# One spectrum tile with two channels interleaved, filled by one copy per step, in a long-convolution and mixture-of-experts kernel

## The chip, the core and the metric

The kernel runs on one core of one Trainium2 chip. The metric is the device time of one execution in microseconds, the median over runs. One execution was also recorded by the hardware profiler; the durations below are from that record. The engines are named as in the profile: PE is TensorE's matmuls and PEld its weight loads, DVE is VectorE, ACT is ScalarE, POOL is GpSimd and SP is SyncE, which issues most DMAs.

## What is computed

For each of four batches of 10048 positions with 128 channels, `u = x * v` is convolved along the positions with a filter that a small network makes, and the result is multiplied by x. Each of the 40192 rows then goes to one of 16 experts.

```python
h_filt = np.maximum(pos_emb @ w1, 0.0) @ w2 * np.exp(-0.01 * pos)[:, None]
Uf = np.fft.rfft(x * v, n=2 * S, axis=1)
Hf = np.fft.rfft(h_filt, n=2 * S, axis=0)
y = np.fft.irfft(Uf * Hf[None], n=2 * S, axis=1)[:, :S, :]
rows = (x * y).reshape(B * S, D)
...
g_idx = np.argmax(rows @ w_group, axis=1)          # a group of experts
e_idx = np.argmax(xg @ w_expert[g], axis=1)        # an expert of the group
ye = np.maximum(xg[mask_e] @ w1[g, e], 0.0) @ w2[g, e]
out[tok_idx] = combined[:, None] * ye
```

## The kernel before

The transform is done in two factors, 157 frequencies by 128 places; by symmetry 79 frequencies (NB) are kept. The work of one batch passes three stages, and each batch's last stage is merged with the next batch's first.

**Forward stage.** `dft_blocks` (L408) works on steps of three channels (GD). One step multiplies the folded input `eo` by the constants `fa` into a PSUM tile `psa`: for each channel two products, one for each half of the partitions. The result holds 158 values per channel, 79 frequencies by two parts. ScalarE copies it to SBUF in two instructions: the lower 64 frequencies (KM) to the tile `z`, 384 elements, and the upper 15 to the tile `zr`, 90 elements. In the filter's own transform and in batch 0, VectorE does some of these copies. What feeds a step is in `product` and `fold`: a DMA loads x and v of three channels (`xv`, five buffers), VectorE multiplies them (L467), ScalarE negates a half (L478), VectorE adds (L480).

**Middle stage.** `middle` and `dft_positions` take two frequencies at a time across all channels (moving operand `z[:, :, k]`, L497), multiply with the filter's spectrum, and `back` (L667) transforms back (L673) and has ScalarE copy the result into the same places of `z` or `zr` (L680).

**Inverse stage.** `turned` (L683) turns twelve channels at a time: three transposes of `zr` (L692), each with four channels' 32 upper values, and twelve of `z` (L695), one for each channel with 128 lower values. They fill four PSUM tiles `pt`, which ScalarE copies to four tiles `tt` (L697). The pool of `pt` has three buffers, so the last four transposes wait until the first `pt` has been copied. `inverse_rest` (L701) multiplies the first `tt` with the constants `fi` into two PSUM tiles `po` (L707), and `inverse_blocks` (L712) adds the products of the other three (L728) for each run of six channels. ScalarE then makes `oo` from `po` in two instructions (L737, L738), VectorE adds (`yt`, L743) and multiplies by x (`xy`, L745).

In the loop of `conv`, the inverse stage of one batch and the forward stage of the next run merged: for each twelve channels, one `turned`, one `inverse_rest`, two `inverse_blocks` and four forward steps. This document calls such a round a **turn**, from one burst of L707 on TensorE to the next. There are ten full turns and a short one in each of the three merged stages, then the last inverse stage of batch 3 without forward steps, then the experts.

Each engine works through its list in order. The lists come from a scheduler, which places an instruction by its dependences; those marked with `keep_in_program_order` (the copies to `z`, the negations L478, VectorE's L467 and L480) keep the order of the code among themselves, while the copies of `pt` and the two `oo` instructions may be placed between them as the scheduler sees fit.

## Time and profile before

| | |
|---|---|
| median of 3 runs | 1946.3 us (1944.04 to 1946.36) |
| the profiled execution | 1945.94 us, its span 1944.2 us |
| PE, PEld busy | 1852.0 us (95%), 1567.9 us (81%) |
| DVE, ACT, POOL busy | 1458.0 us (75%), 1317.4 us (68%), 1086.7 us (56%) |
| forward stage of the filter, of batch 0 | about 43 to 78 us, 118 to 178 us |
| merged stages | about 247 to 341, 440 to 535 and 643 to 742 us |
| last inverse stage | about 848 to 912 us, then the experts to the end |

A busy share is a mean over stages with different limits, and the records of neighbouring matmuls overlap, so that TensorE can show as busy while nothing new is issued. For a stage that repeats, the time from one start of the same instruction to the next says more: it contains every wait. The timeline views give those starts.

### The profile page before, as it was taken

The page shows a single profiled execution, that of the slowest core. Times are in us where ns is not written, and L with a number is a line of the kernel's source. Part 1 is how long each engine was busy: PE and PEld are TensorE (multiplying, and loading weights), DVE is VectorE, ACT ScalarE, POOL GpSimd, SP SyncE. Part 2 cuts the span into 40 slices and gives each one's busy share as a digit, 9 for nine tenths or more (in the row PEclk, how much of TensorE's full clock was granted, in tenths as well). Part 3 has the DMA queues.
Part 4 walks back from the last instruction along what each step waited for, and adds up shares of the span by engine and source line. Part 5 has one row for each costly group of instructions (what it writes and reads, how often), then busy time and mean ns, then how long its engine had stood idle before and what let it go on. Part 6 is the DMA issues. An engine that isn't in the chain of part 4 may idle for free.

```text
span 1944.2 us, 44476 instructions
## 1 busy us (share of the span) xinstructions
PE 1852.0 (95%) x14494; PEld 1567.9 (81%) x14494; DVE 1458.0 (75%) x3102; ACT 1317.4 (68%) x3017; POOL 1086.7 (56%) x1225
## 2 busy tenths in 40 slices
PE   8988999989999899978899999999999999999997
PEld 7966878778877687766788888888888888899997
DVE  6577767688768976893789777777777777778885
ACT  6653378447843685446777777777777777788886
POOL 3237710664799568967255556666664333355554
PEclk9999999999999999999899999999999999999999
DMA  4599976988998799857653344444343222234332
GB/s 145 199 283 252 306 188 191 350 267 263 282 326 289 233 265 343 302 186 241 218 194 112 118 128 127 164 133 131 121 131 98 90 94 97 79 119 128 122 121 77
DMA packets 234433, 365.19 MB, mean 188 GB/s; under 512 B 29687, under 2 KB 113634, under 8 KB 234192
## 3 DMA queue, kind: packets, MB, share of 16 engines
q1 hardware_dynamic: 198960, 286.90, 47.9%
q0 software_dynamic: 25728, 59.82, 8.9%
q10 hardware_dynamic: 9504, 15.54, 2.9%
q8 instruction: 117, 1.92, 0.4%
q14 instruction: 124, 1.02, 0.2%
HBM read 272.15 MB, written 91.03 MB: 187 GB/s over the span
## 4 chain that ended last, share of the span: by engine, by line
PE 66%; DVE 10%; DMA 4%; ACT 4%; issue 3%; POOL 2%; SPq 0%; ACTq 0%; DVEq 0%; POOLq 0%
PE ph L1334 8%; PE ph L1336 8%; PE py L1354 8%; PE ph L1335 8%; PE py L1356 8%; PE py L1355 8%; PE psb L497 4%; PE pbp L673 3%; PE ptm L1368 2%; PE px L1289 2%; PE po L728 2%; DMA xv<-xv_in 2%; PE po L707 2%; DMA bt<-c_b 1%; DVE t L660 1%
## 5 line engine op out<-in xcount | busy, mean ns | idle before, releaser
L1343 DVE SCALAR_TENSOR_TENSOR hl<-ph,hh 128x512 fp32r<-128x512 f32 x656 | 450.4, 687 | 172.1 <-ACT hh L1342 167.2
L1380 POOL DMA_INDIRECT out<-os,to x328 | 324.6, 990 | 384.1 <-ACT os L1375 309.6
L1342 ACT ACTIVATE hh<-ph 128x512 fp32r<-128x512 f32 x656 | 395.4, 603 | 157.5 <-PE ph L1336 134.8
L378 POOL DMA_INDIRECT prow<-stg,adr x316 | 326.3, 1032 | 122.6 <-issue 53.9
L1334 PE MATMUL ph<-xh,wh 128*128 128x512 f32 (+1 forms) x808 | 301.2, 373 | 2.2 <-ACT wh L1316 2.2
L1336 PE MATMUL ph<-xh,wl 128*128 128x512 f32 (+1 forms) x808 | 284.4, 352 | 0.0
L1354 PE MATMUL py<-hh,wh 128*128 128x512 f32 (+1 forms) x808 | 283.5, 351 | 0.0
L1335 PE MATMUL ph<-xl,wh 128*128 128x512 f32 (+1 forms) x808 | 283.4, 351 | 0.0
L1356 PE MATMUL py<-hh,wl 128*128 128x512 f32 (+1 forms) x808 | 283.0, 350 | 0.0
L1355 PE MATMUL py<-hl,wh 128*128 128x512 f32 (+1 forms) x808 | 282.2, 349 | 0.0
L661 POOL TENSOR_TENSOR y<-t 128x256 f32<-128x256 f32 (+1 forms) x160 | 121.1, 757 | 141.0 <-DVE t L660 136.4
L412 PE MATMUL psa<-fa,eo 96*64 96x158 f32 x2048 | 182.1, 305 | 12.6 <-POOL eo L486 5.7
L680 ACT COPY z<-pbp 128x512 f32<-128x512 f32 x128 | 74.8, 585 | 160.5 <-PE pbp L673 155.7
L673 PE MATMUL pbp<-y,bp 128*128 128x256 f32 x632 | 164.7, 384 | 12.7 <-POOL y L664 12.7
L497 PE MATMUL psb<-z,bt 128*128 128x256 f32 x640 | 161.8, 384 | 10.6 <-DMA bt<-c_b 3.9
L1336 PEld LDWEIGHTS ph<-xh,wl 128*128 128x128 f32 x808 | 153.6, 190 | 21.2 <-DVE wl L1323 0.2
L1355 PEld LDWEIGHTS py<-hl,wh 128*128 128x128 f32 x808 | 153.2, 190 | 20.9
L1356 PEld LDWEIGHTS py<-hh,wl 128*128 128x128 f32 x808 | 153.1, 189 | 20.7
L1354 PEld LDWEIGHTS py<-hh,wh 128*128 128x128 f32 x808 | 153.0, 189 | 20.3
L412 PEld LDWEIGHTS psa<-fa,eo 96*64 96x64 f32 x2048 | 143.2, 138 | 32.0 <-POOL eo L486 9.2
L1334 PEld LDWEIGHTS ph<-xh,wh 128*128 128x128 f32 x808 | 154.0, 191 | 17.3 <-ACT wh L1316 2.4
L1335 PEld LDWEIGHTS ph<-xl,wh 128*128 128x128 f32 x808 | 154.5, 191 | 14.9
(233 smaller groups left out, 3771.4 us busy)
## 6 DMA issues: line engine op xcount, KB each, us to landing
ws<-m_w SPq DMA_DIRECT2D x202, 256.0 KB
ht<-hspec SPq DMA_DIRECT2D x156, 256.0 KB
xv<-xv_in SPq DMA_DIRECT2D x131, 288.0 KB
bt<-c_b SPq DMA_DIRECT2D x95, 256.0 KB
bp<-c_bp SPq DMA_DIRECT2D x76, 256.0 KB
xyd<-xy SPq DMA_DIRECT2D x76, 256.0 KB
stg<-xyd SPq DMA_DIRECT2D x76, 256.0 KB
xg<-prow SPq DMA_DIRECT2D x63, 260.0 KB
```

The costliest lines, as they stand in the source:

```text
L378: ins = self.nc.gpsimd.indirect_dma_start(self.d["prow"], bass.IndirectOffsetOnAxis(ap=u.adr[:, t : t + 1], axis=0), u.rows[:, t - u.t0], ...
L412: ins = nc.tensor.matmul(ps[hs, i], eo[:, i, hs], self.fa[:, h], start=True, stop=True)
L497: nc.tensor.matmul(ps[:, i].rearrange("p s d -> p d s"), bt[:, i], self.frequency(k0 + i, 1)[:, :, 0], start=True, stop=True,)
L1334: k.fix(nc.tensor.matmul(ph[:, j], wh, self.xh, start=True, stop=False))
L1335: k.fix(nc.tensor.matmul(ph[:, j], wh, self.xl, start=False, stop=False))
L1336: k.fix(nc.tensor.matmul(ph[:, j], wl, self.xh, start=False, stop=True))
L1342: k.fix(nc.scalar.activation(hh, ph, AF.Relu))
L1343: k.fix(nc.vector.scalar_tensor_tensor(hl, ph, 0.0, hh.bitcast(F32), ALU.max, ALU.subtract))
L1354: k.fix(nc.tensor.matmul(self.py, wh, hh, start=(c == 0), stop=False))
L1355: k.fix(nc.tensor.matmul(self.py, wh, hl, start=False, stop=False))
L1356: k.fix(nc.tensor.matmul(self.py, wl, hh, start=False, stop=(c == NC - 1)))
L1380: ins = k.nc.gpsimd.indirect_dma_start(k.d["out"], bass.IndirectOffsetOnAxis(ap=self.to[:, h : h + 1], axis=0), o, None, bounds_check=k.nt ...
```

## The change

`z` and `zr` become one tile of 64 channel pairs by 160 values by two channels, so that a channel's neighbouring values stand 8 bytes apart. A forward step now covers one of the two places of its pairs and needs one copy of 3 x 158 elements instead of two. So that steps pair up, the last eight channels are done in four steps of two instead of two of three and one of two: 44 steps instead of 43. The upper values of a pair are interleaved now and are turned by ordinary products with the identity, two for each place of `pt`, each giving 64 partitions: six products instead of three transposes per turn. The transposes of the lower values read their weights with a step of two elements. `dft_positions` and `back` read and write runs of 4 and 8 elements instead of 2 and 4. The constants `fi` and the order of the channels on the host follow.

```diff
-        self.z = zp.tile([128, D, KM, 2], F32, name="z")
-        self.zr = zp.tile([128, D, 16, 2], F32, name="zr")
-        nc.vector.memset(self.zr[:, :, NB - KM :], 0.0)
+        self.z = zp.tile([128, D // 2, 2 * KM + 32, 2], F32, name="z")
+        nc.vector.memset(self.z[:, :, 2 * NB :], 0.0)
...
+PARTS = groups(120, GD) + [(d0, 2) for d0 in range(120, 128, 2)]
...
-        for name, to, at in (
-            ("z", main, ps[:, :n, : 2 * KM]),
-            ("zr", rest, ps[:, :n, 2 * KM :]),
-        ):
-            ins = copy(to, at)
+        pair = d0 // (2 * n) * n
+        ins = copy(self.z[:, pair : pair + n, : 2 * NB, d0 // n % 2], ps[:, :n])
...
-                ps[:, i].rearrange("p s d -> p d s"),
+                ps[:, i].rearrange("p s (a t) -> p a s t", t=2),
                 bt[:, i],
-                self.frequency(k0 + i, 1)[:, :, 0],
+                self.frequency(k0 + i, 1),
...
-        for s, m in [(None, n // 4)] + groups(n, 4):
+        m = n // 4
+        for g in range(-1, m):
             pt = self.psT.tile([128, 4, 128], F32, tag="pt", name="pt")
-            for i in range(m):
-                if s is None:
-                    src = self.zr[:, d0 + 4 * i : d0 + 4 * i + 4].rearrange("p d k s -> p (d k s)")
-                    nc.tensor.transpose(pt[:, i], src, self.ident)
+            for i in range(m if g < 0 else 4):
+                if g < 0:
+                    for run, rs in enumerate(HALVES):
+                        src = self.z[:, d0 // 2 + run * m + i, 2 * KM :].rearrange("p k t -> p (k t)")
+                        nc.tensor.matmul(pt[rs, i], src, self.ident, start=True, stop=True)
                 else:
-                    src = self.z[:, d0 + s + i].rearrange("p k s -> p (k s)")
+                    src = self.z[:, d0 // 2 + i // 2 * m + g, : 2 * KM, i % 2]
                     nc.tensor.transpose(pt[:, i], src, self.ident)
```

The code around the merged loop is the same, but the scheduler gives the lists another order. ScalarE's list in the first merged stage, between the `oo` of a turn's first run (first two rows) and the copies of the next `pt`; before, from every second turn (xv is the negation L478, z and zr the copies of a forward step):

```order
L737 ACTIVATE oo<-po 64x474
L738 COPY oo<-po 64x474
L478 ACTIVATE xv<-xv 96x3x64
L425 COPY z<-psa 128x384
L425 COPY zr<-psa 128x3x30
L737 ACTIVATE oo<-po 64x474
L738 COPY oo<-po 64x474
L478 ACTIVATE xv<-xv 96x3x64
L425 COPY z<-psa 128x384
L425 COPY zr<-psa 128x3x30
L478 ACTIVATE xv<-xv 96x3x64
```

In the turns between, the list before has the order that the changed kernel has in every turn of this stage:

```order
L737 ACTIVATE oo<-po 64x474
L738 COPY oo<-po 64x474
L478 ACTIVATE xv<-xv 96x3x64
L424 COPY z<-psa 128x3x158
L723 DMA xo<-x_out 128x474
L478 ACTIVATE xv<-xv 96x3x64
L424 COPY z<-psa 128x3x158
L737 ACTIVATE oo<-po 64x474
L738 COPY oo<-po 64x474
L478 ACTIVATE xv<-xv 96x3x64
L424 COPY z<-psa 128x3x158
L697 COPY tt<-pt 128x384
```

The second run's `oo` has moved behind the second negation of the turn. TensorE's list in the same stage, before, for two turns from the transposes on (psa are the forward products, po with 64x158 the burst L707):

```order
L692 MATMUL pt<-ident,zr 128x128 x3
L695 MATMUL pt<-ident,z 128x128 x8
L412 MATMUL psa<-fa,eo 64x158 x5
L695 MATMUL pt<-ident,z 128x128 x4
L412 MATMUL psa<-fa,eo 64x158
L707 MATMUL po<-fi,tt 64x158 x12
L728 MATMUL po<-fi,tt 64x79 x12
L412 MATMUL psa<-fa,eo 64x158 x12
L728 MATMUL po<-fi,tt 64x79 x12
L412 MATMUL psa<-fa,eo 64x158 x6
L692 MATMUL pt<-ident,zr 128x128 x3
L695 MATMUL pt<-ident,z 128x128 x8
```

And in the changed kernel, where eight turns of the first merged stage read alike:

```order
L692 MATMUL pt<-ident,z 64x128 x6
L695 MATMUL pt<-ident,z 128x128 x8
L416 MATMUL psa<-fa,eo 64x158 x5
L695 MATMUL pt<-ident,z 128x128 x4
L416 MATMUL psa<-fa,eo 64x158
L707 MATMUL po<-fi,tt 64x158 x12
L728 MATMUL po<-fi,tt 64x79 x12
L416 MATMUL psa<-fa,eo 64x158 x12
```

Before, every second turn has nine forward products ahead of the last four transposes and none behind them; now every one of these eight has five ahead and one behind. The ninth has three and three. In the second merged stage one turn has three and three, one five and one, and seven have seven ahead and none behind; in the third, four have seven ahead, one five and one, and the first half is irregular as before. At the end of each merged stage the last copy to `z`, on which the next L497 waits, now stands behind the last two `oo` instructions on ScalarE; before it stood ahead of them. 

## Rows read from the trace of the kernel before

**Rows 1.** Busy time by stretch: PE, PEld, DVE, ACT, POOL, clock, DMA share, GB/s.

```profile
250.00:330.00 80.00, 76.97 (x1227) 66.26 (x1225) 56.20 (x106) 66.23 (x181) 0.00 (x0) 1.00 0.67 182
445.00:530.00 85.00, 81.00 (x1274) 69.94 (x1270) 68.15 (x141) 68.69 (x187) 54.05 (x57) 0.98 0.97 280
645.00:735.00 90.00, 84.99 (x1309) 72.22 (x1309) 74.28 (x172) 69.38 (x187) 56.23 (x52) 0.99 0.95 261
```

**Rows 2.** Timeline of TensorE, two turns: start, length, line, operation, count, idle before.

```profile
268.82 1.04 PE L707 MATMUL po<-fi,tt 64*64 64x158 f32 x24
...
276.29 0.66 PE L695 MATMUL pt<-ident,z 128*128 128x128 f32 x4 [0.19 <-ACT tt L697]
276.87 0.48 PE L412 MATMUL psa<-fa,eo 96*64 96x158 f32 x2
277.29 1.04 PE L707 MATMUL po<-fi,tt 64*64 64x158 f32 x24
...
282.46 0.55 PE L692 MATMUL pt<-ident,zr 128*128 128x128 f32 x3
...
285.76 0.66 PE L695 MATMUL pt<-ident,z 128*128 128x128 f32 x4 [0.39 <-ACT tt L697]
286.35 0.90 PE L707 MATMUL po<-fi,tt 64*64 64x158 f32 x20
```

**Rows 3.** Timeline of ScalarE in the second of these turns.

```profile
279.40 0.56 ACT L737 ACTIVATE oo<-po 64x474 f32<-64x474 f32 x1 [0.95 <-PE po L728]
279.98 0.55 ACT L738 COPY oo<-po 64x474 f32<-64x474 f32 x1
...
282.44 0.36 ACT L478 ACTIVATE xv<-xv 96x192 f32<-96x192 f32 x1 [1.03 <-DVE xv L467]
282.71 0.46 ACT L425 COPY z<-psa 128x384 f32<-128x384 f32 x1
283.07 0.23 ACT L425 COPY zr<-psa 128x90 f32<-128x90 f32 x1
283.33 0.56 ACT L737 ACTIVATE oo<-po 64x474 f32<-64x474 f32 x1
...
285.10 0.23 ACT L425 COPY zr<-psa 128x90 f32<-128x90 f32 x1
285.23 1.94 ACT L697 COPY tt<-pt 128x384 f32<-128x384 f32 x4
```

**Rows 4.** Timeline of VectorE there, ahead of the negation at 282.44.

```profile
281.24 0.65 DVE L745 TENSOR_TENSOR xy<-yt,xo 128x474 f32<-128x474 f32 x1
```

**Rows 5.** Timeline of ScalarE in the first of the two turns.

```profile
273.09 0.56 ACT L737 ACTIVATE oo<-po 64x474 f32<-64x474 f32 x1
```

**Rows 6.** Groups by line, 0 to 1100 us: busy us, mean ns, idle before and releasers.

```profile
L497 PE MATMUL psb<-z,bt 128*128 128x256 f32 x640 | 161.8, 384 | 10.6 <-DMA bt<-c_b 3.9 <-DVE hs L635 2.4 <-DVE t L663 2.2
L425 ACT COPY z<-psa 128x384 f32<-128x384 f32 x181 | 85.3, 471 | 55.3 <-PE psa L412 55.1
L425 ACT COPY zr<-psa 128x90 f32<-128x90 f32 x181 | 43.7, 241 | 0.0
```

**Rows 7.** One line's instructions, L866: shortest/median/longest ns; it writes every second element.

```profile
L866 DVE TENSOR_SCALAR en<-idc x4: 193/458/797, 414.0 to 1008.0; 128x79 f32<-128x79 f32 x4
```

**Rows 8.** Timeline of TensorE in the last inverse stage.

```profile
879.36 1.04 PE L695 MATMUL pt<-ident,z 128*128 128x128 f32 x8
881.10 0.66 PE L695 MATMUL pt<-ident,z 128*128 128x128 f32 x4 [0.70 <-ACT tt L697]
```

**Rows 9.** Timeline of TensorE and ScalarE at the end of the first merged stage.

```profile
341.25 2.88 PE L497 MATMUL psb<-z,bt 128*128 128x256 f32 x12
...
341.34 0.43 ACT L737 ACTIVATE oo<-po 64x316 f32<-64x316 f32 x1
```

**Rows 10.** Timeline of TensorE, forward products of a step group in the same stage.

```profile
279.12 1.78 PE L412 MATMUL psa<-fa,eo 96*64 96x158 f32 x24
280.74 0.99 PE L728 MATMUL po<-fi,tt 128*64 128x79 f32 x24
```

More of the change, by code (lines that the diff above doesn't have):

```diff
@@ L98, in make_consts @@
         both[:NB, 1 - swap] = (2 * swap - 1) * w * np.sin(ang)
-        rest = np.zeros((4, 32, 2, NB))
-        for i in range(4):
-            rest[i, :, i % 2] = both[KM:].reshape(32, NB)
+        rest = np.zeros((2, 32, 2, 2, NB))
+        for i in range(2):
+            rest[:, :, i, i] = both[KM:].reshape(32, NB)
         sign = 1 - 2 * swap
@@ L138, with step_of @@
 OUTS = groups(120, GI) + [(120, 4), (124, 4)]
+PARTS = groups(120, GD) + [(d0, 2) for d0 in range(120, 128, 2)]
+def step_of(d0):
+    return d0 // GD if d0 < 120 else 40 + (d0 - 120) // 2
 def channels():
     order = []
-    for i, (d0, n) in enumerate(OUTS):
-        first = d0 - i % 2 * n
-        order += [first + 4 * (c // 2) + i % 2 * 2 + c % 2 for c in range(n)]
+    for d0, n in OUTS:
+        order += [d0 + c % 2 * (n // 2) + c // 2 for c in range(n)]
     return np.array(order)
@@ L247, in conv @@
                 xy = xyp.tile([128, NB, D], F32, tag="xy", name=f"xy{b - 1}")
-            parts = groups(D, GD) if not last else []
+            parts = PARTS if not last else []
             if b == 1:
@@ L406, in dft_blocks @@
         nc = self.nc
-        pool, tag = (self.psA, "ps") if b not in ("h", 0) or d0 // GD % 2 else (self.psT, "pt")
+        pool, tag = (self.psA, "ps") if b not in ("h", 0) or step_of(d0) % 2 else (self.psT, "pt")
         ps = pool.tile([128, GD, 2 * NB], F32, tag=tag, name="psa")
@@ L417, in dft_blocks @@
         copy = nc.vector.tensor_copy if other else nc.scalar.copy
-        main = self.z[:, d0 : d0 + n].rearrange("p d k s -> p d (k s)")
-        rest = self.zr[:, d0 : d0 + n].rearrange("p d k s -> p d (k s)")[:, :, : 2 * (NB - KM)]
-        for name, to, at in (
-            ("z", main, ps[:, :n, : 2 * KM]),
-            ("zr", rest, ps[:, :n, 2 * KM :]),
-        ):
-            ins = copy(to, at)
-            self.in_turn(b, ins)
-            self.tc.declare_no_dep(ins.ins, group=f"{name}{b}", reason="every step has channels of its own")
-            self.tc.add_to_no_dep_group(f"{name}{b}", ins.ins)
+        pair = d0 // (2 * n) * n
+        ins = copy(self.z[:, pair : pair + n, : 2 * NB, d0 // n % 2], ps[:, :n])
+        self.in_turn(b, ins)
+        self.tc.declare_no_dep(ins.ins, group=f"z{b}", reason="every step has channels of its own")
+        self.tc.add_to_no_dep_group(f"z{b}", ins.ins)
         self.pace = ins
     def run_ahead(self, b, i, made, folded):
-        parts = groups(D, GD) if b < self.nbat else []
+        parts = PARTS if b < self.nbat else []
         while len(made) < min(len(parts), i + AHEAD + 2):
@@ L488, in fold @@
         self.in_turn(b, sub.tensor_tensor(eo[:, :n, 64:128], lo, hi, ALU.subtract))
-        return b, eo, d0, n, d0 // GD % 5 == 4 or d0 // GD == 41
+        return b, eo, d0, n, step_of(d0) % 5 == 4 or d0 == 124
     def dft_positions(self, k0, n, bt, other=False):
@@ L506, in frequency @@
     def frequency(self, k, n):
-        z, k = (self.z, k) if k < KM else (self.zr, k - KM)
-        return z[:, :, k : k + n]
+        return self.z[:, :, 2 * k : 2 * (k + n)]
     def parts(self, pool, src, tag, bufs=1, lo=None):
@@ L598, in filter @@
                 break
-        for d0, n in groups(D - FH, GD):
-            self.dft_blocks("h", eo[1][:, d0 : d0 + n], FH + d0, n, d0 // GD % 2 > 0)
+        for d0, n in (p for p in PARTS if p[0] >= FH):
+            self.dft_blocks("h", eo[1][:, d0 - FH : d0 - FH + n], d0, n, step_of(d0) % 2 == 0)
         halves[1].close()
@@ L679, in back @@
             )
-        self.pace = nc.scalar.copy(self.frequency(k0, n), po[:, :, :n])
+        self.pace = nc.scalar.copy(self.frequency(k0, n), po[:, :, : 2 * n])
     def turned(self, d0, n):
```

22 lines of the change are left out of this document (11 added, 11 removed).

## The prediction

> **What bounds the kernel now.** The change touches the forward copies, the middle stage's operands and the transposes. I read the busy shares by stretch first. In the three merged stages TensorE shows 77 of 80, 81 of 85 and 85 of 90 us [rows 1], ScalarE 66 to 69 and VectorE 56 to 74. By that table TensorE is the bound, but its records overlap, so I went to the timelines and asked how long one turn takes and what it is made of.
>
> A turn from one L707 burst to the next takes 8.47 us (268.82 to 277.29) and the following one 9.06 (277.29 to 286.35) [rows 2], and the two alternate, 8.77 on the mean. The long turn can be taken apart without a remainder, along a loop through three engines. From L707 it is 2.11 us until ScalarE starts the first run's `oo` (279.40), behind L728. From there 3.04 us to the second negation at 282.44, which waited 1.03 us for VectorE [rows 3]: VectorE had to wait for `oo`, then add and multiply (L745 at 281.24, [rows 4]) before the product that the negation reads. Then 0.89 us for negation, z and zr, 1.90 us for the second run's `oo`, a negation, z and zr, and 0.53 us until the first `pt` is copied and its buffer free (285.23 to 285.76) [rows 3, 2]. The last four transposes start there, and L707 follows 0.59 us later. 2.11 + 3.04 + 0.89 + 1.90 + 0.53 + 0.59 = 9.06. TensorE itself stands idle for 0.39 us before the four transposes, more than that behind the modelled ends.
>
> In the short turn ScalarE does the second run's `oo` before that negation: it starts 4.27 us after L707 (273.09) [rows 5, 2], against 6.04 in the long one (283.33). VectorE's work then hides behind `oo`, and this pays for the 1.00 us from transposes to L707 (276.29 to 277.29), where a forward product stands between. So a turn is bound by the loop, not by any engine's sum, and the two lists of ScalarE in the section on the change are its two versions.
>
> **The change part by part.** The forward copies: z and zr take 471 and 241 ns on the mean, 181 times on ScalarE [rows 6]. The slope between 384 and 90 elements is 0.78 ns, so 474 elements take about 0.54 us; an `oo` copy of 474 takes 0.55 [rows 3], and I take that. Busy time falls by 0.16 us a step. What the loop gains is less, since a copy overlaps the one before: z and zr take 0.62 us from start to start up to `oo` (282.71 to 283.33) and 0.49 up to the `pt` copy (0.36 and 0.13) [rows 3]. One copy would take 0.58 and 0.43. The two copies that lie on the loop save 0.04 and 0.06, the other two of a turn lie in waits. A long turn becomes 8.96.
>
> The order: every turn of the changed kernel has ScalarE's long-turn order. That costs 8.96 - 8.77 = 0.19 us a turn by itself. Where one forward product stands behind the four transposes, L707 follows 1.00 instead of 0.59 us after their start, so 9.37; with three, four more records of 67 ns (24 in 1.62 us, 279.12 to 280.74, [rows 10]) make it 9.64. First merged stage: eight turns of 9.37 and one of 9.64, 8 x 0.60 + 0.87 = 5.7 us. Second: seven of 8.96 and one of 9.37, 7 x 0.19 + 0.60 = 1.9; the one with three falls in a turn that waits for VectorE anyway. Third: 4 x 0.19 + 0.60 = 1.4; for its irregular half I take nothing. Sum 9.0 us. The bounds are 4 us, if the product behind the transposes costs nothing, and 12, if the irregular turns pay too.
>
> The products with the identity: a single-pass transpose takes about 0.10 us ((1.04 - 0.55) / 5, from eight and three in a burst, [rows 8, 2]), so three take 0.3. Six float products are recorded as twelve; L412, also on half the columns each, makes 67 ns for 158 columns, so 54 for 128 and 0.65 in all: 0.35 us more per turn. This lies beside the loop. From L707 to the turn's L692 it is 5.17 us (277.29 to 282.46); with 0.65 for the products, 0.9 for eight transposes and 0.7 to 0.9 for forward products TensorE reaches the last four transposes at 7.4 to 7.7 us, while the loop lets them go at 8.37. In the last inverse stage TensorE idles 0.70 us at that point [rows 8], which covers it too. Without that cover it would cost 0.35 x 42 turns, 15 us. It has no cover at the four starts of these stages, where L692 waits for the last copy of the middle stage: 1.4 us.
>
> The Trainium skill, page "TensorE: Matmul & The Clock Gate", section "Terms", speaks against this part: it says that the transpose mode is four times as fast for FP32 as not using it. By it the six products would take up to 1.3 us per turn with two halves side by side, about 1 us more than the transposes, and the sum would be some 8 us higher.
>
> The end of a merged stage: L497 starts at 341.25, ahead of the last `oo` at 341.34 (0.43 us, two of them) [rows 9]. Now the copy that it waits for comes behind them, so it starts up to 0.9 us later, three times. What follows is partly bound by VectorE's routing work, so I take half, 1.4 us; the ends are 0 and 2.7.
>
> The rest I cost at nothing. The filter's forward stage is bound by TensorE's unchanged products, batch 0 by loads. L497 reads its moving operand in runs of two elements at present, and twelve of its records follow each other in 2.88 us [rows 9], 0.23 us for 256 columns less the last one's 0.38; that is 0.9 ns a column, near the 0.8 of the transposes with contiguous operands, so longer runs have little to gain and I take nothing. The 44th step's extra negation, copy and load lie in waits; uncovered, about 1 us a batch.
>
> Weights with a step of two elements and copies that write every second element are not in this trace in just that form. The nearest row is L866, where VectorE writes every second element: 79 elements in 193 ns at best, 458 at the median [rows 7], so a full rate is possible and a loss not excluded. L497's moving operand, in runs of two at wide steps, is read at full rate [rows 6]. I take no loss. Upper bound, double time per element: 0.4 us for each of the two copies on the loop, 0.8 x 30 = 24 us, and 0.1 us for each of the four transposes on it, 13 us there and 4 in the last stage.
>
> The Trainium skill, page "SBUF — State Buffer", section "Door 1: The DMA port swizzle", gives lines of 16 bytes and full bandwidth when two accesses fall in one line, as with a step of two fp32. By that rule this loss would have a chance of 0.03 rather than the 0.10 below; the median of L866 does not bear it out clearly.
>
> Sum against the profiled execution, 1945.94 us: 9.0 + 1.4 + 1.4 = 11.8, so 1957.7; I say 1958. That execution lies 0.4 us below the median of the runs.
>
> **Rivals.** *ScalarE's sum sets the turn (faster).* If ScalarE's list were what limits the merged stages, all 129 pairs of copies there would return their 0.16 us: -21 us, 1925, or about 1938 with the order's cost on top. It decides only if ScalarE has no waits left in a turn. For it: ScalarE works without idle time from `oo` to the copies in the short turn. Against it: 0.95 and 1.03 us of idle time in the long one [rows 3]. Chance 0.16, between 1925 and 1941.
>
> *The order hardly matters (no change).* If TensorE started L707 beside the forward product, all turns would take 8.96, 22 x 0.19 = 4 us more; with the ends of the stages absorbed and a little gained elsewhere, 1943 to 1950. The short turn's 1.00 us speaks against it. Chance 0.13.
>
> *Every second element is dear.* 1974 (weights alone) to 1999. Chance 0.10.
>
> *The products outgrow their cover.* If they took twice as long, 1.3 us, TensorE would reach the last transposes at 8.1 to 8.4 us with the same forward products and later where these wait: up to 0.3 us in 30 turns, 9 us, and 0.3 in ten of the last stage, 1960 to 1970. The page's factor for the transpose mode would be that case. Twelve records of L412's kind [rows 10] speak against it. Chance 0.05.
>
> **How the numbers follow.** The forecast, 1951 to 1965, has 0.56. Slower by over 0.2% (3.9 us, about what a measurement here can tell from no change) are the forecast, the dear elements and the products: 0.71. Within: 0.13. Faster: 0.16. The range 1940 to 1974 holds the forecast, no change, the products' case, the upper edge of the faster case and the lower edge of the dear elements, some 0.8.
>
> **What would show it.** The turns of the first merged stage at 9.37 us each without alternation, those of the second at 8.96; the second negation waiting over 1 us for L467 in each; the forward copy at 0.55 us; transposes still at 0.10 to 0.11 us apart, L692's twelve in 0.65; the last inverse stage's turns unchanged. Turns below 8.77 would overthrow the loop; turns of 9.06 behind a forward product would overthrow the 0.41; a copy of 0.9 us or transposes 0.2 apart would show the dear elements.

## The result, and the profile after

The changed kernel takes 1966.86 us (median of 4 runs, 1961.41 to 1971.23), the kernel before 1945.17 us beside it (4 runs, 1942.9 to 1946.36): a ratio of 1.0106, with a 95% interval of 1.0077 to 1.0135. It is slower, as forecast, and by more than the 11.8 us of the sum: 2 us above the 1951 to 1965 of the forecast and inside the 1940 to 1974 of the range. The profiled execution is the slowest of the four, 1971.23 us with a span of 1969.4.

To see where the time went I cut both spans at the first and the last record of L707 in each merged stage. The column "again" is a second trace of the same changed kernel (first experiment below).

| stretch | before | after | difference | difference, again | predicted |
|---|---|---|---|---|---|
| start to first L707 | 250.80 | 252.07 | +1.27 | +3.12 | +0.35 |
| first merged stage | 87.52 | 94.21 | +6.69 | +6.69 | +5.7 |
| middle | 104.45 | 104.04 | -0.41 | -0.53 | +0.8 |
| second merged stage | 90.34 | 95.25 | +4.91 | +6.84 | +1.9 |
| middle | 113.25 | 113.28 | +0.03 | +2.01 | +0.8 |
| third merged stage | 93.31 | 104.54 | +11.23 | +0.98 | +1.4 |
| middle | 108.24 | 108.77 | +0.53 | +0.48 | +0.8 |
| last inverse stage | 63.72 | 64.87 | +1.15 | +0.37 | 0 |
| rest | 1032.56 | 1032.37 | -0.19 | -0.16 | 0 |
| span | 1944.2 | 1969.4 | +25.2 | +19.8 | +11.8 |

Busy shares tell little of this. The row of busy times on the page, after (us, share of the span, instructions):

```profile
PE 1878.1 (95%) x14878; PEld 1601.0 (81%) x14878; DVE 1459.9 (74%) x3080; ACT 1314.5 (67%) x2840; POOL 1086.8 (55%) x1226
```

TensorE's share is what it was, and ScalarE has 177 instructions less but only 2.9 us less of busy time. The turns do tell it. TensorE's timeline of one turn of the first merged stage, after (start, length, engine, line, operation, count, idle time before it and what ended that):

```profile
289.98 1.04 PE L707 MATMUL po<-fi,tt 64*64 64x158 f32 x24
...
295.05 0.83 PE L692 MATMUL pt<-ident,z 128*64 128x128 f32 x12
295.81 1.23 PE L695 MATMUL pt<-ident,z 128*128 128x128 f32 x8
296.97 1.02 PE L416 MATMUL psa<-fa,eo 96*64 96x158 f32 x10
298.38 0.74 PE L695 MATMUL pt<-ident,z 128*128 128x128 f32 x4 [0.40 <-ACT tt L697]
299.06 0.48 PE L416 MATMUL psa<-fa,eo 96*64 96x158 f32 x2
```

And ScalarE's in the same turn:

```profile
292.09 0.56 ACT L737 ACTIVATE oo<-po 64x474 f32<-64x474 f32 x1 [1.03 <-PE po L728]
...
295.13 0.36 ACT L478 ACTIVATE xv<-xv 96x192 f32<-96x192 f32 x1 [1.04 <-DVE xv L467]
295.39 0.58 ACT L424 COPY z<-psa 128x474 f32<-128x474 f32 x1
295.99 0.57 ACT L737 ACTIVATE oo<-po 64x474 f32<-64x474 f32 x1
...
297.87 1.94 ACT L697 COPY tt<-pt 128x384 f32<-128x384 f32 x4
```

This is the long turn of [rows 2, 3] once more, in the same steps: 2.11 from L707 to the first `oo` (292.09), 3.04 to the second negation (295.13, which waited 1.04 us for VectorE, as 1.03 before), 0.86 to the second run's `oo`, 1.88 to the copy of `pt`, 0.51 to the last four transposes, and 1.09 to the next L707 at 299.47. The sum is 9.49. In the first merged stage seven turns take 9.49 to 9.52 without alternation, and one, with three products behind the transposes, 9.77; in the second, where none stands there, the regular turns take 9.10. TensorE waits 0.40 us ahead of the last transposes, so the six products with the identity still had cover.

The third merged stage is another matter. Busy time and granted clock by stretch (columns as in [rows 1]), of the changed kernel's first trace:

```profile
686.00:704.00 18.00, 18.00 (x151) 13.84 (x149) 11.51 (x25) 6.37 (x15) 0.83 (x3) 0.54 0.54 167
```

For these 18 us the granted clock was 0.54, close to the lower of the two levels (1.2 of 2.4 GHz), and TensorE shows as busy all the time with 8.4 records a us, where a second trace of the same kernel has 13.1 in nearly the same stretch (first experiment below). Ahead of it TensorE had waited for VectorE:

```profile
684.45 2.47 PE L416 MATMUL psa<-fa,eo 96*64 96x158 f32 x24 [1.64 <-DVE eo L480]
```

### The profile page after: what moved, and what is told of

It is laid out like the page before. It is cut to its first block, busy times and chain, and to the rows that moved or that the text cites. A ratio compares the mean times of both kernels' runs of the same rounds, so it can differ in the third digit from the quotient of the medians.

```text
span 1969.4 us, 45039 instructions
## 1 busy us (share of the span) xinstructions
PE 1878.1 (95%) x14878; PEld 1601.0 (81%) x14878; DVE 1459.9 (74%) x3080; ACT 1314.5 (67%) x2840; POOL 1086.8 (55%) x1226
## 4 chain that ended last, share of the span: by engine, by line
PE 50%; issue 1%; ACT 1%; DMA 1%; DVE 0%; POOL 0%; SPq 0%; ACTq 0%; POOLq 0%; DVEq 0%
PE ph L1334 8%; PE py L1354 8%; PE py L1356 8%; PE ph L1336 8%; PE py L1355 8%; PE ph L1335 8%; PE ptm L1368 2%; PE px L1289 2%; DMA wf<-m_w 1%; PE ptr L810 1%; PE plt L818 0%; PE pl L835 0%; PE po L728 0%; PE po L707 0%; ACT oo L738 0%
## 5 line engine op out<-in xcount | busy, mean ns | idle before, releaser
L678 ACT COPY z<-pbp 128x512 f32<-128x512 f32 (+1 forms) x160 | 92.2, 579 | 199.8 <-PE pbp L671 199.7
L497 PE MATMUL psb<-z,bt 128*128 128x256 f32 x790 | 202.5, 387 | 19.0 <-DMA bt<-c_b 5.4
L416 PE MATMUL psa<-fa,eo 96*64 96x158 f32 x2048 | 187.4, 313 | 12.0 <-POOL eo L486 5.2
L497 PEld LDWEIGHTS psb<-z,bt 128*128 128x128 f32 x790 | 146.6, 196 | 47.0 <-issue 11.3
L416 PEld LDWEIGHTS psa<-fa,eo 96*64 96x64 f32 x2048 | 147.9, 142 | 28.4 <-POOL eo L486 7.9
```

The source lines that it names most:

```text
L416: ins = nc.tensor.matmul(ps[hs, i], eo[:, i, hs], self.fa[:, h], start=True, stop=True)
L497: nc.tensor.matmul(ps[:, i].rearrange("p s (a t) -> p a s t", t=2), bt[:, i], self.frequency(k0 + i, 1), start=True, stop=True,)
```

## The experiments

The theory under test: a turn is as long as the loop through ScalarE, VectorE and TensorE, and ScalarE's order decides which loop that is. Rivals: the order hardly matters, and the slowdown comes from TensorE's added work (the products, the step of two) as a sum; or from the new copies.

**The same kernel again.**

> The changed kernel once more, nothing altered. The turns of the first two merged stages are set by instruction order, so they should return within 0.02 us (9.50 with a forward product behind the last four transposes, 9.10 without). The irregular half of the third stage held 18 us at a granted clock of about half in the trace of the changed kernel, 12.28 and 17.73 us for two turns; if that is an accident of one execution, it is gone or smaller here and the time lies near 1962; if it belongs to the change, it returns and the time lies at 1966 to 1971.

It took 1965.06 us against 1947.14 of the kernel before, ratio 1.0085 (1.0060 to 1.0109). The turns of the first stage are the same within 0.02 us, those of the second without a product behind the transposes 9.10 to 9.15. In the third stage the row for nearly the same stretch as above is

```profile
684.00:704.00 20.00, 18.94 (x262) 15.64 (x258) 19.81 (x49) 14.35 (x32) 1.83 (x4) 1.00 0.81 241
```

and the stage takes 94.29, 0.98 more than before. TensorE's wait for VectorE is there again, 1.06 us where it was 1.64:

```profile
687.53 1.89 PE L416 MATMUL psa<-fa,eo 96*64 96x158 f32 x24 [1.06 <-DVE eo L480]
```

So 10 of the 25 us between the first two traces did not come back with the same kernel; the runs' spread from 1961 to 1971 is of that size. The time is not the 1962 of the expectation all the same: here the second stage is 1.9 us longer than in the first trace (one L707 burst, at 484.07, took 1.86 us instead of 1.04), and the second middle stage 2.0, at whose end the first transposes of the third stage to its first L707 take 5.84 us, where the first trace has 3.40.

**The order alone, in the kernel before.** Each `oo` is bound to come behind the last copy to `z` written ahead of it, so that all turns get ScalarE's long order. Layout and copies are the old ones.

```diff
-        nc.scalar.activation(oo[0:64], by_row[64:128], AF.Copy, scale=-1.0)
+        ins = nc.scalar.activation(oo[0:64], by_row[64:128], AF.Copy, scale=-1.0)
+        if b < self.nbat - 1:
+            self.after(ins, self.pace)
```

> The kernel before, with its old layout and its two copies, and one edit: each oo is bound to come behind the last copy to z written ahead of it, so that every turn of the merged stages has ScalarE's long-turn order. Loop theory: no short turns of 8.47 are left, all regular turns take 9.06 (here twelve forward products stand ahead of the last four transposes and none behind): 0.59 x 4 in the first stage, as much in the second, half in the third, 6 us, 1951 (1949 to 1954). Rival, that the order hardly matters: 1945 within 2 us, with turns still at 8.77 on the mean.

1954.22 us (10 runs) against 1947.14, ratio 1.0039 (1.0024 to 1.0053): 7 us slower. All regular turns take 9.05 or 9.06. ScalarE's and TensorE's timeline in one of them:

```profile
289.14 0.56 ACT L737 ACTIVATE oo<-po 64x474 f32<-64x474 f32 x1 [0.54 <-PE po L728]
...
292.19 0.36 ACT L478 ACTIVATE xv<-xv 96x192 f32<-96x192 f32 x1 [1.03 <-DVE xv L467]
...
293.07 0.56 ACT L737 ACTIVATE oo<-po 64x474 f32<-64x474 f32 x1
```

```profile
287.03 1.04 PE L707 MATMUL po<-fi,tt 64*64 64x158 f32 x24
...
295.50 0.66 PE L695 MATMUL pt<-ident,z 128*128 128x128 f32 x4 [0.82 <-ACT tt L697]
296.08 1.04 PE L707 MATMUL po<-fi,tt 64*64 64x158 f32 x24
```

Here twelve forward products stand ahead of the last transposes, and TensorE still waits 0.82 us: the engine with the highest busy share has time to spare. The first stage is 2.66 us longer than before, the second 4.42, of which its first four turns make half, 40.7 us instead of 38.5. That the order lengthens these irregular turns, too, is what the prediction left out; of the one turn there it said that it "falls in a turn that waits for VectorE anyway".

**The short order, in the changed kernel.** The second run's products and `oo` are written ahead of the step before them; VectorE's part (`late`) stays where it was.

```diff
+                if b > 0 and j % 2 and not last:
+                    late = self.inverse_blocks(b - 1, xy, d0, n, tts, pos[1], 1)
                 for i in range(2 * j, min(2 * j + 2, len(parts))):
                     self.run_ahead(b, i, made, folded)
...
-                        self.inverse_blocks(b - 1, xy, d0, n, tts, pos[j % 2], j % 2)
+                        if j % 2 == 0:
+                            late = self.inverse_blocks(b - 1, xy, d0, n, tts, pos[0], 0)
+                        late()
...
+        def late():
+            ...
+        return late
```

> The changed kernel, with one edit: in the merged stages the second run's inverse products and its two oo instructions are written ahead of the step before them, so that ScalarE does both oo pairs with one negation and one copy between them in every turn (the short turn's order), and VectorE's adding and multiplying for the second run stays where it was. Loop theory: the second oo starts 4.0 us after L707 (1.04 + 1.07 + 0.81 for six products + 1.07), from there 3.1 to the last four transposes, then 1.54 with five products behind them: 8.65 us a turn instead of 9.50 and 9.10. TensorE's own sum (3.24 for 24 forward products, 1.04, 2.1, 1.6 for twelve transposes, 0.76 for the six products with the identity) is about as long, so 8.7. That is 0.8 x 8 in the first stage, 0.4 x 6 in the second, about 2 in the third: 11 us below the changed kernel, 1955 where that takes 1966. Rival, that the added work on TensorE and the stride are the cause and the order hardly matters: turns stay at 9.1 to 9.5 and the time within 3 us of the changed kernel.

1956.07 us (10 runs), ratio to before 1.0044 (1.0029 to 1.0059): 9 us below the 1965.06 of the changed kernel on the same chip. The turns shorten as expected, but to 9.03, not 8.65. Its rows:

```profile
288.37 1.03 PE L711 MATMUL po<-fi,tt 64*64 64x158 f32 x24
...
295.36 0.48 PE L420 MATMUL psa<-fa,eo 96*64 96x158 f32 x2
295.78 0.75 PE L699 MATMUL pt<-ident,z 128*128 128x128 f32 x4
296.46 1.02 PE L420 MATMUL psa<-fa,eo 96*64 96x158 f32 x10
297.40 1.04 PE L711 MATMUL po<-fi,tt 64*64 64x158 f32 x24
```

```profile
290.49 0.56 ACT L741 ACTIVATE oo<-po 64x474 f32<-64x474 f32 x1 [1.40 <-PE po L732]
...
292.52 0.56 ACT L741 ACTIVATE oo<-po 64x474 f32<-64x474 f32 x1
...
295.22 1.98 ACT L701 COPY tt<-pt 128x384 f32<-128x384 f32 x4
```

The loop is 2.12 from L711 to the first `oo`, 4.73 to the copy of `pt` (ScalarE without a wait), 0.56 to the last transposes, 1.62 to L711 with five products between: 9.03. I had the parts from L707 to the second `oo` at 4.0 (4.15 here) and the other two at 3.1 (3.26) and 1.54. TensorE shows no idle time either. Its last four transposes start 0.23 us after the record ahead of them; where transposes wait for the copy of `pt`, in both kernels and in before_long, that distance is 0.48 to 1.12 us, and they start 0.51 to 0.55 after the copy's start. So here TensorE's own sum came last, by some 0.03 us, and the loop is nearly as long.

**The step of two alone.** The transposes read 128 adjacent values of a pair; the list of instructions is that of the changed kernel.

```diff
-                    src = self.z[:, d0 // 2 + i // 2 * m + g, : 2 * KM, i % 2]
+                    src = self.z[:, d0 // 2 + i // 2 * m + g, :KM].rearrange("p k t -> p (k t)")
```

> The changed kernel, with the transposes of the lower frequencies reading 128 adjacent values of a pair instead of every second one; this takes other data than the reference wants, and the order of all instructions is the same as in the changed kernel. Only the step of two is taken away. If the step of two in the stationary operand is what spreads the transposes from 0.109 to 0.133 us, they return to 0.11. Loop theory: only the last four lie on the loop, 0.10 us in some 24 turns of the merged stages, and 0.08 in the ten of the last inverse stage: 3 us less, turns of 9.40 and 9.00. Rival, that TensorE's sum sets the turns: 12 x 0.024 = 0.29 us in all 34 turns, 10 us less.

Turns of 9.41 to 9.43 instead of 9.50, 9.02 instead of 9.10, 5.47 instead of 5.55 in the last inverse stage. The rows that answer to those of the changed kernel:

```profile
285.41 1.09 PE L695 MATMUL pt<-ident,z 128*128 128x128 f32 x8
...
287.99 0.66 PE L695 MATMUL pt<-ident,z 128*128 128x128 f32 x4 [0.54 <-ACT tt L697]
```

Eight transposes take 1.09 instead of 1.23 and four 0.66 instead of 0.74, some 0.02 us each for the step of two. A turn loses only the 0.09 of the last four; the 0.14 of the eight turns up as a longer wait (0.54 instead of 0.40). That is the loop's sign, against the rival's 0.29. Other data are routed here, so the time of the whole run, 1979.82 us, is not compared.

**The products with the identity alone.** Three transposes of adjacent values stand in their place, and the long order is bound as in the run before_long.

```diff
-                    for run, rs in enumerate(HALVES):
-                        src = self.z[:, d0 // 2 + run * m + i, 2 * KM :].rearrange("p k t -> p (k t)")
-                        nc.tensor.matmul(pt[rs, i], src, self.ident, start=True, stop=True)
+                    src = self.z[:, d0 // 2 + i, KM + 32 :].rearrange("p k t -> p (k t)")
+                    nc.tensor.transpose(pt[:, i], src, self.ident)
```

> The changed kernel with three transposes of 128 adjacent values in place of the six products with the identity, which takes other data than the reference wants, and with the long turn's order on ScalarE bound by hand in every turn, as the changed kernel has it. Loop theory: the six products lie beside the loop, so regular turns with no product behind the last transposes stay at 9.05 to 9.10; only the wait ahead of those transposes grows, from 0.40 to about 0.8 us. Rival, that the products had outgrown their cover: 8.7. The end to end time is not comparable, since other data are routed.

Turns of 9.10 to 9.12, as in the changed kernel without a product behind the transposes. The wait ahead of the transposes grows:

```profile
294.39 0.55 PE L691 MATMUL pt<-ident,z 128*128 128x128 f32 x3
294.77 1.12 PE L694 MATMUL pt<-ident,z 128*128 128x128 f32 x8
...
298.44 0.75 PE L694 MATMUL pt<-ident,z 128*128 128x128 f32 x4 [0.78 <-ACT tt L696]
```

Three transposes take 0.38 from start to start (294.39 to 294.77) where the six products took 0.76. The saving went into the wait, 0.78 instead of 0.40 (and 0.41 in after_ahead2 below, with as many forward products between L707 and these transposes as here). In the long order the products cost nothing.

**The short order, in the kernel before,** by the diff of order_short; and a second version (before_p), in which the last four transposes are bound behind the six forward products of the step and L707 directly behind them:

```diff
                     self.dft_blocks(*folded[i])
...
+                            self.turned(d0, min(2 * GI, D - d0), tts, True)
                             pos = self.inverse_rest(min(2 * GI, D - d0), tts)
...
-                    nc.tensor.transpose(pt[:, i], src, self.ident)
+                    ins = nc.tensor.transpose(pt[:, i], src, self.ident)
+                    if late and i == 0:
+                        self.tc.keep_in_program_order(ins)
```

> The kernel before, with its old layout and its two copies, and the edit of the run called order_short: the short turn's order on ScalarE in every turn. Loop theory: every regular turn takes what the short turns take, 8.47, in place of 8.77 on the mean (five forward products stand ahead of the last four transposes and one behind). TensorE's own sum is below that: 9.03 without idle time in order_short, less 0.38 for three transposes in place of six products (0.76 against 0.38 from the first to the next group) and less 0.28 for twelve transposes at 0.109, so 8.37. That is 0.59 us less in each of five turns in the first stage, as much in the second, half in the third, 6 us: 1941 where the kernel before takes 1947. Rival, that the order hardly matters: 1947 within 2 us.

> As before_short, with one more edit: the last four transposes of a turn are bound to come behind the six forward products of the step, and L707 directly behind these transposes, so that no product stands between them and L707. Loop theory: 0.41 us less on the loop, 8.06, which is below TensorE's own sum of 8.37, so TensorE becomes the bound and a turn takes 8.3 to 8.4: 22 turns with 0.4 us less than 8.77, 9 us, 1938. Rival: the last copy to tt now stands behind a negation and a copy on ScalarE, and L728 waits for it; turns then stay at 8.5 or above and the time at 1941 or more.

before_short: 1942.73 us (12 runs) against 1945.71 (23 runs), ratio 0.9979 (0.9968 to 0.9991); every regular turn 8.47 or 8.48. That is the expected number, but not for the expected reason:

```profile
293.50 1.02 PE L416 MATMUL psa<-fa,eo 96*64 96x158 f32 x10
294.45 0.66 PE L699 MATMUL pt<-ident,z 128*128 128x128 f32 x4
295.04 0.48 PE L416 MATMUL psa<-fa,eo 96*64 96x158 f32 x2
295.45 1.03 PE L711 MATMUL po<-fi,tt 64*64 64x158 f32 x24
```

```profile
293.82 1.96 ACT L701 COPY tt<-pt 128x384 f32<-128x384 f32 x4
```

The transposes start 0.63 us after the copy of `pt`, not 0.53, and without a wait behind the forward products. The loop would give 2.12 + 4.73 + 0.53 + 1.00 = 8.38; TensorE's own sum, 8.48, sets the turn.

before_p: 1941.91 us, 0.9977 (0.9967 to 0.9988); every regular turn 8.07 to 8.09. It has the lowest median here, though these runs do not tell it from before_short. TensorE became the bound, as expected: the transposes start 0.64 us after the copy of `pt` (290.17 to 290.81 below). But the turn is 8.07, not 8.3 to 8.4. My 8.37 came from order_short, whose list cuts a step's six forward products into five and one; in that list the sum is 8.48. Uncut, the six take 0.95 us (289.86 to 290.81 below); five alone take as much (293.50 to 294.45 above) and the one 0.41 more (295.04 to 295.45). The rows of before_p:

```profile
283.32 1.04 PE L715 MATMUL po<-fi,tt 64*64 64x158 f32 x24
...
288.50 0.55 PE L699 MATMUL pt<-ident,zr 128*128 128x128 f32 x3
288.89 1.04 PE L702 MATMUL pt<-ident,z 128*128 128x128 f32 x8
289.86 1.03 PE L419 MATMUL psa<-fa,eo 96*64 96x158 f32 x12
290.81 0.66 PE L702 MATMUL pt<-ident,z 128*128 128x128 f32 x4
291.40 1.04 PE L715 MATMUL po<-fi,tt 64*64 64x158 f32 x24
```

```profile
290.17 1.45 ACT L706 COPY tt<-pt 128x384 f32<-128x384 f32 x3
```

The gain end to end is 4 us where the turns promised 9. Between the two traces (spans of 1937.1 and 1944.2, 7 apart where the medians are 4) the first merged stage is 6.8 shorter, the third 2.1, the second only 0.8: its second and third turn are longer, 12.99 and 9.71 instead of 11.36 and 8.84, and so is its last but one, 9.45 instead of 8.46. The last of the three middle stages is 2.3 longer. Why that one grew I did not test; it is as long in order_short and before_short, and not in before_long.

**TensorE's work of before in the new layout's order.** order_short with the edits of contiguous and three_long.

> order_short with TensorE's work of the kernel before: transposes that read 128 adjacent values, and three of them in place of the six products with the identity; this takes other data than the reference wants. ScalarE keeps the one forward copy per step. If TensorE's sum is what held order_short at 9.03, a turn falls to what the loop then gives, 2.12 to the first oo + 4.73 to the copy of pt + 0.53 + 1.27 with three products behind the last transposes = 8.65. If the copies that write every second element or something else held it, 9.0 stays. The end to end time is not comparable, since other data are routed.

One execution. The regular turns take 8.61 to 8.63, with three products behind the last transposes; expected were 8.65. Here the transposes wait for the copy of `pt` again and start 0.53 us after it:

```profile
291.28 0.75 PE L420 MATMUL psa<-fa,eo 96*64 96x158 f32 x6
292.12 0.66 PE L698 MATMUL pt<-ident,z 128*128 128x128 f32 x4
```

```profile
291.59 1.93 ACT L700 COPY tt<-pt 128x384 f32<-128x384 f32 x4
```

So the loop sets this turn, while order_short, with the longer work on TensorE, stood at TensorE's sum, 9.03; its loop alone would have given 2.12 + 4.73 + 0.53 + 1.62 = 9.00. The copies with a step of two, the same in both, held neither.

**The best order in the new layout, first attempt.**

> The changed kernel's layout with the orders of before_p: ScalarE has the short turn's order in every turn, six forward products stand ahead of the last four transposes, and L707 directly behind them (here every group of products on TensorE is bound to the order of the program, which gives the same list as before_p). From the trace of order_short the loop is 2.12 to the first oo + 4.73 to the copy of pt + 0.56 to the last transposes + 0.68 to L707 = 8.09. TensorE's own sum is the 8.07 of before_p, less at most 0.1 of idle time there, plus 0.38 for six products in place of three transposes and 0.28 for the step of two: 8.63. Theory that a turn is the longer of the loop and TensorE's sum: 8.6, that is 0.5 us a turn more than before_p, about 10 us in all, 1951 where before_p takes 1942. Rival, that the layout costs nothing beside the order: 8.1 as in before_p, 1942. Rival, that the copies and the products already held order_short at 9.03: no turn below 9.0, 1956.

> The changed kernel with ScalarE's order as it is (the long turn's in every turn), but with the six forward products of a step ahead of the last four transposes in every turn and L707 directly behind these transposes; every group of products on TensorE is bound to the order of the program. Loop theory: the turns of the first merged stage lose the product between transposes and L707, 0.40 us, and take 9.10 like those of the second: 9 x 0.4 = 3.6 us in the first stage and one turn of 0.4 in each of the others, 4 us, 1960 to 1962. Rival, that the product there costs nothing since TensorE has to do it somewhere: 9.50 stays.

Both runs are lost for the question. In the new layout a pair holds channels of two steps, so the last four transposes read pairs that the step ahead of them writes. I had put the step as a whole, with its copy to `z`, ahead of these transposes; they then waited for the copy and read the new values, another computation than the reference. Turns came to 9.73 and 10.80. What stays is that the interleaved layout ties that step's copy to these transposes, while in before_p neither waits for the other. (These two runs and the next two were on chips on which the kernel before took 2159.8 and 2133.5 us; what grew there are the stages after the first merged one, so across chips I compare that stage alone.)

**Second attempt, with the copy behind the transposes.**

```diff
-                    self.dft_blocks(*folded[i])
+                    held = b > 0 and i % 2 == j % 2 == 0
+                    copy = self.dft_blocks(*folded[i], later=held)
...
+                            self.turned(d0, min(2 * GI, D - d0), tts, True)
                             pos = self.inverse_rest(min(2 * GI, D - d0), tts)
+                            copy()
```

> The changed kernel's layout with the orders of before_p: ScalarE has the short turn's order in every turn, six forward products stand ahead of the last four transposes and L707 directly behind these, and the copy of that step to z stands behind them, since it writes pairs that they still read. Every group of products on TensorE is bound to the order of the program, in the irregular halves too, which may cost there. From the trace of order_short the loop is 2.12 to the first oo + 4.73 to the copy of pt + 0.56 to the last transposes + 0.68 to L707 = 8.09. TensorE's own sum is the 8.07 of before_p, less at most 0.1 of idle time there, plus 0.38 for six products in place of three transposes and 0.28 for the step of two: 8.63. Theory that a turn is the longer of the loop and TensorE's sum: 8.6 in the regular turns, 0.5 more than before_p; the first merged stage takes 85.5. Rival, that the layout costs nothing beside the order: 8.1 as in before_p, 81 for the first stage. Rival, that the copies and products already held order_short at 9.03: no turn below 9.0, 89 for the first stage.

> The changed kernel with ScalarE's order between oo, negations and copies as it is (the long turn's in every turn), but with the six forward products of a step ahead of the last four transposes in every turn and L707 directly behind these; every group of products on TensorE is bound to the order of the program, in the irregular halves too, which may cost there. Loop theory: the turns of the first merged stage lose the product between transposes and L707, 0.40 us, and take 9.10 like those of the second, 3.6 us less in that stage. Rival, that the product there costs nothing since TensorE has to do it somewhere: 9.50 stays.

after_p2: every regular turn of the first merged stage takes 8.62, the stage 85.71, as expected (8.63, 85.5). End to end the ratio to the kernel before is 1.0063 (1.0043 to 1.0083), although the first stage is shorter than the 87.52 of the kernel before; that kernel left no trace on this chip, so where the rest goes is not shown. Rows:

```profile
288.08 1.04 PE L724 MATMUL po<-fi,tt 64*64 64x158 f32 x24
...
293.16 0.83 PE L706 MATMUL pt<-ident,z 128*64 128x128 f32 x12
293.91 1.23 PE L711 MATMUL pt<-ident,z 128*128 128x128 f32 x8
295.07 1.03 PE L425 MATMUL psa<-fa,eo 96*64 96x158 f32 x12
296.03 0.74 PE L711 MATMUL pt<-ident,z 128*128 128x128 f32 x4
296.70 1.04 PE L724 MATMUL po<-fi,tt 64*64 64x158 f32 x24
```

```profile
294.91 1.44 ACT L715 COPY tt<-pt 128x384 f32<-128x384 f32 x3
```

Here TensorE is the bound. The copy of `pt` starts at 294.91, so its buffer is free at about 295.45 (0.53 later, as elsewhere), while TensorE reaches the transposes only at 296.03. Against before_p the same list of work is 0.55 us longer a turn: 0.36 for the products (293.16 to 293.91 against 288.50 to 288.89), 0.19 for eight transposes (1.16 against 0.97 from start to start), 0.08 for four (0.67 against 0.59). That is 0.63; about 0.1 comes back between the forward products and the group behind them. Against the 9.03 of order_short, with the same work on TensorE, the uncut step saves 0.41.

after_ahead2: the turns of the first stage take 9.09 to 9.12 instead of 9.50, the stage 90.40 instead of 94.21. The product between the transposes and L707 costs its 0.40 in full. End to end the ratio is 1.0067 (1.0037 to 1.0098); what the bound order costs in the irregular turns is not separated in it.

## Why the prediction was right, point by point

- **What bounds a turn.** Right. The loop was foreseen as 2.11 + 3.04 + 0.85 + 1.84 + 0.53 + 1.00 = 9.37 and measured as 2.11 + 3.04 + 0.86 + 1.88 + 0.51 + 1.09 = 9.49. In before_long the order alone gives the 9.06 foreseen, to 0.01 us. That before_short gives 8.47 was luck: there TensorE's sum sets the turn, and the loop would give 8.38. No engine's busy share shows any of this.
- **The order as the cause.** Right for the first stage, and it can be split there: 2.7 us for the long order in every turn (before_long), 3.8 for the product behind the transposes (94.21 against 90.40, the latter from another chip), and 0.2 for all that the layout itself does in that order (90.40 against 90.18).
- **The size of a turn, +0.13.** The step "I take no loss" for weights with a step of two failed by a little: 0.02 us a transpose, 0.09 on the loop. The copy takes 0.57 to 0.59 where I took 0.55. Nine turns make 1.1 us, about the difference between 5.7 and 6.69. The same 0.08 a turn appears in the last inverse stage (5.55 instead of 5.47), which I had costed at nothing. The Trainium skill, page "SBUF — State Buffer", section "Door 1: The DMA port swizzle", lets a step of two fp32 run at full bandwidth; the measured 0.02 us a transpose is a small loss that the rule doesn't have, and far from the doubled time of the upper bound. The longer runs of L497's operand brought nothing, as costed: its median is 379 ns, 377 before.
- **The forward copies.** "Busy time falls by 0.16 us a step" was wrong, though not on the loop. The two copies overlapped, so that means of 471 and 241 ns [rows 6] do not add; the page's busy time of ScalarE fell by 2.9 us in 181 steps, 0.016 each. So the first rival had no such sum to return even if ScalarE had set the turn.
- **The products with the identity.** Right that they have cover: the wait is 0.40 with them and 0.78 without. They take 0.76 to the next group, not 0.65, against 0.38 for three transposes. The Trainium skill, page "TensorE: Matmul & The Clock Gate", section "Terms", gives a factor of four for the transpose mode; these traces show a factor of two, for six products on half the columns each in place of three transposes. The rival "products outgrow their cover" gave 1960 to 1970, where the measured time lies; it is the waits, not the time, that speak against it. It has its place after all in orders that I did not consider: with the short order TensorE is the bound, and the products and the step of two make the turn 8.62 in place of 8.07.
- **The second and third merged stages.** Mis-sized. I had 1.9 for the second and measured 4.9 and 6.8. The regular turns make 3.0 of it (63.4 against 60.4 in the last seven) and the irregular first three 2.0 (31.4 against 29.4), where I had let the order cost nothing; before_long shows the same excess without the new layout. Of the 11.2 us of the third stage 0.98 came back in the second trace, where 1.4 was foreseen; whether the change makes the stretch at the lower clock more likely is not shown.
- **Starts and ends.** The mechanism was right, but its cost hardly shows in the table. At the first start, from the first transposes to L707, the kernel takes 3.40 us instead of 2.74, 0.66 more where I took 0.35. L497 waits behind the last `oo`, more than I took:

```profile
350.44 1.13 PE L497 MATMUL psb<-z,bt 128*128 128x256 f32 x4 [1.01 <-ACT z L424]
```

  It starts 4.16 us after the start of the last record of L707 instead of 2.92 [rows 9], 1.24 or 1.25 later in each of the three stages; yet the first middle stage as a whole is 0.4 shorter. At the start of the second merged stage a part of that shows: the group of transposes there ran at a granted clock of 0.68 before and at 1.00 after (columns as in [rows 1]).

The kernel before:

```profile
438.80:442.70 3.90, 3.84 (x27) 3.52 (x27) 3.90 (x20) 2.40 (x6) 1.14 (x1) 0.68 0.65 224
```

The changed kernel:

```profile
446.90:450.30 3.40, 3.38 (x36) 2.88 (x36) 3.40 (x18) 2.27 (x5) 1.33 (x1) 1.00 0.84 276
```

  Together the three middle stages, for which 2.4 us were foreseen, changed by 0.15 us in the first trace and by 1.96 in the second, while the second merged stage brought 3.0 and 4.9 more than foreseen. So misses in both directions partly cancelled in the total, which is luck.
- **What stays open.** The start to the first L707 varied between 249.6 and 254.3 us over all traces here, so its +1.27 is not assigned. The two ratios give 16.6 and 20.6 us. Of these the order in the kernel before explains 7 and the products behind the transposes about 4.6 (3.8 and one turn of 0.4 in each of the two other stages); the rest, 5 to 9 us, was not split further; the irregular turns, the last stage and stretches at the lower clock are where the table above has it. Why the scheduler arrives at other lists for this layout was not looked into.

## What to carry to other kernels

A change of layout can cost more through the order that a scheduler then chooses than through its own instructions, so read the lists of both kernels and take one turn apart, start to start, into the loop that closes it; where TensorE shows a wait, the loop's sums held here to 0.13 us, while busy shares and means of overlapping instructions misled. Where it shows none, its own list is the bound, and the order counts there, too: a step cut in two cost 0.41 us. Work that has cover costs nothing only as long as the loop is the bound: with the loop shortened, the same products and strides cost 0.55 us a turn. And before one judges a layout, bind the order by hand in both kernels; the best version here is the old layout with a bound order, 0.23% faster than before.

## What the runs showed of the hardware that I had not expected

**A product without its partner takes TensorE as long as two.** Each forward product is recorded twice. The records of two products, one for each half of the partitions, start 0.006 us apart and the next two 0.13 us later; those of a product alone stand 0.13 us apart, too (before, 284.94 and 285.07). So the ten records of five products take 0.94 us up to L711 (order_short, 296.46 to 297.40) where the twelve of six take 0.95 up to the next transposes (before_p, 289.86 to 290.81), and the sixth product by itself costs 0.41 more, its two changes of shape included.

**Groups of another shape cost TensorE a pause.** The forward products work on 96 by 64, the transposes on 128 by 128, L728 on 128 by 64. Twelve forward records take 0.95 us between two groups of transposes, as above, but 24 take 1.62 between products of L728 [rows 10], 0.81 for twelve: 0.14 us for the change of shape and back, counted from start to start. The Trainium skill, page "TensorEngine Tiling (Array Packing)", section "Key Properties", says that a change of tiling mode drains TensorE; a pause at the change agrees with it, and that the array drains there is not shown by these runs.

**A short wait can be followed by a long stretch at the lower clock.** In one execution of the changed kernel 18 us of the third merged stage ran at a granted clock of 0.54 behind a wait of 1.64 us, and in another execution, with a wait of 1.06 us at the same place, the clock stayed at 1.00. Between the two lie 10 us, more than the order's 7. That the wait is the cause was not tested.
